# Batch 0's q of a linear-attention and expert-branch kernel: one load for each pair of heads in 1024-byte pieces, turned by products on column halves, and new durations in the planner

## The chip, the cores and the metric

The kernel runs on one core of a Trainium2 chip. The metric is the device time in microseconds (us) of one execution; times given for a kernel are the median of several executions. Engines are named as in the profile: PE is TensorE's matmul side, PEld its weight loads, DVE is VectorE, ACT is ScalarE, POOL is GpSimd, and SP is SyncE, which issues most of the DMAs.

## What is computed

```python
# q, k, v: (8 batches, 8 heads, 576 rows, 64)
kv  = np.einsum('bhsd,bhse->bhde', k, v)
out = np.einsum('bhsd,bhde->bhse', q, kv)
rms = np.sqrt(np.mean(out * out, axis=-1, keepdims=True) + 1e-06)
out = out / rms * g_norm
x = out.transpose(0, 2, 1, 3).reshape(4608, 512)
p = domain_probs / (domain_probs.sum(-1, keepdims=True) + 1e-09)   # (4608, 4)
y = sum over e of p[:, e:e+1] * (np.maximum(x @ w1[e], 0) @ w2[e])  # w1: 512x1024, w2: 1024x512
```

All of it is in float32. Attention without a softmax comes first: for each head a 64x64 product of keys and values, then the queries times it, then a normalisation over the 64 columns. Four expert branches follow, each an up product, a ReLU and a down product, mixed by the normalised domain probabilities.

## The kernel before

**The work.** The 4608 rows are cut into nine chunks of 512: the first 512 rows of each of the eight batches, and one chunk of the eight remainders of 64 rows. A stage s is one branch e on one chunk c. A stage has an up part and a down part; nearly all of them are done with a scheme of seven products of half-size blocks, nested twice, so that VectorE, ScalarE and GpSimd form many sums and differences (`combine`, L360). Stage 0 alone has a plain up part (`up_plain`, products at L999), for which only x of batch 0 and w1 of branch 0 are needed. The attention of batch 0 runs before stage 0, that of batch c+1 beside stage c.

**The attention of one batch** works on four pairs of heads. `load_pair` (from L611) loads q, k and v of a pair. For q it issues one DMA for each of the two heads: partition p gets rows 4p to 4p+3, and the two heads lie side by side inside each row block, so a row's 64 numbers, 256 bytes, are one piece. k and v are one DMA each for both heads, with 1536-byte pieces on 96 partitions. `turn` (L651) makes four 128x128 transposes on TensorE, which gives q turned with head 0 on partitions 0 to 63 and head 1 on 64 to 127; ScalarE copies that out of PSUM (L656). `key_values` (L665) makes the 64x64 products for both heads, each head in its own half of the columns; ScalarE copies them (L678). `attend` (L691) multiplies, `scaled` normalises (ScalarE squares at L564, VectorE sums at L571, GpSimd takes the power at L578 and L582, VectorE multiplies at L591), and `turn_x` (L709, copied at L717) turns the result into the layout of the products. Batch 0 has its pairs one by one, the others in two groups of two pairs. The 64 remainder rows of a batch follow the same way (L735 to L779).

**The order** is made by a planner, `Plan.layout`, before the kernel is built. Each operation has a key, which says when it is wanted, and a cost for each engine that can do it, in us. `layout` walks a clock and gives each free engine an operation. TensorE and SyncE take the first in the order of keys that can start, within a reach (0.7 of a key for TensorE); the others take the one that is due first. An operation on another engine can start 0.3 after what it needs has ended. A load ends when a modelled bus has moved it: the bus begins at 3.0 us and moves 215 KB per us, 0.5 us later the data count as landed, and at most eight loads are under way. Tiles and PSUM banks are taken from pools ("ab" and "db" have two banks each) and given back when their last reader has ended. When TensorE finds nothing to start and the first key still open on it is below 0.0, the planner adds a filler, `idle` (two transposes of the identity, L1353), with a cost of 0.23, from 1.6 us on. The order that comes out is fixed: on the chip each engine runs its list in order and waits only for semaphores. So the planner's numbers decide the order and the number of fillers, and not how long anything takes.

**The loads of branch 0's w1** are four DMAs of 512 KB (`weights_1`, from L431) in 2048-byte pieces. SyncE issues them after batch 0's q, k and v and before batch 1's.

Of the kernel before, what the change touches and what calls it, by code (L numbers as in the profile page):

```python
# [34 lines left out]
class Plan:  # L35
# [13 lines left out]

    SPARE = {"big": 6, "small": 3}  # L50
    STEP, LATE = 44.0, 20.0

    def __init__(self):
        self.ops = []
# [26 lines left out]
    def layout(self, slots, later, idle, idle_banks, idle_until):  # L81
# [20 lines left out]
                cross = self.SAME if op.cost.keys() == d.cost.keys() else self.CROSS  # L102
                d.due = min(d.due, op.due - cross - min(d.cost.values()))
        busy = {e: 0.0 for e in todo}
        bus, port = 3.0, 0.0
        lanes = [0.0] * self.LANES
        t = 0.0
        wake = [0.0, 1.6]
# [24 lines left out]
        while left:  # L133
            moved = False
            while todo["PE"] and todo["PE"][0].start is not None:
                todo["PE"].pop(0)
            front = todo["PE"][0].key if todo["PE"] else 1e9
            for eng in todo:
                if busy[eng] > t:
                    continue  # L140
                pending = todo[eng]
                while pending and pending[0].start is not None:
                    pending.pop(0)
                if not pending:
                    continue
                reach = pending[0].key + self.REACH[eng]
                best = None
                for op in pending:
                    if op.key > reach:
                        break  # L150
                    if op.start is not None:
                        continue
                    if best is not None and op.due >= best.due:
                        continue
                    when = ready(op, eng)
                    if when is None:
                        continue
                    if when > t:
                        heapq.heappush(wake, when)
                        continue  # L160
                    best = op
                    if eng in ("PE", "SP"):
                        break
                if best is not None:
                    op = best
                    op.start, op.eng = t, eng
                    if eng == "SP":
                        busy[eng] = t + op.cost[eng]
                        bus = max(bus, t + 1.5) + op.kb / 215.0
                        op.end = bus + 0.5  # L170
                        lanes = lanes[1:] + [op.end]
                    else:
                        op.end = busy[eng] = t + op.cost[eng]
                        if op.kb:
                            op.end += 9.0 if op.kb == 512 else 5.5
                    if op.port:
                        port = op.end
                        heapq.heappush(wake, port)
                    for b in op.outs:
                        if b.kind is not None and b.slot is None:  # L180
                            free[b.kind].sort()
                            b.slot = free[b.kind].pop(0)[1]
                            b.ap = slots[b.kind][b.slot]
                    for b in op.bufs:
                        b.left -= 1
                        if b.left == 0 and b.kind is not None:
                            end = max(o.end for o in [op] + b.readers + b.writers) + self.CROSS
                            free[b.kind].append((end, b.slot))
                            live[b.kind] -= 1
                            ended[b.kind] = max(end, ended.get(b.kind, 0.0))  # L190
                            for rule in [r for r in later if not any(live.get(k) for k in r[0])]:
                                later.remove(rule)
                                end = max(ended[k] for k in rule[0])
                                for ap in rule[2]:
                                    free.setdefault(rule[1], []).append((end, len(slots[rule[1]])))
                                    slots[rule[1]].append(ap)
                                heapq.heappush(wake, end)
                    heapq.heappush(wake, busy[eng])
                    heapq.heappush(wake, op.end + self.SAME)
                    heapq.heappush(wake, op.end + self.CROSS)  # L200
                    order.append(op)
                    left -= 1
                    moved = True
                if eng == "PE" and busy[eng] <= t and 1.6 <= t and front < idle_until:
                    kind, spare = next((
                        (k, f) for k in idle_banks for f in free[k] if f[0] <= t
                    ), (None, None))
                    if spare is not None:
                        op = Op(front, {"PE": 0.23}, None, (), (), 0, False)
                        op.start, op.eng, op.end = t, eng, t + 0.23  # L210
                        op.fn = lambda eng, bank=slots[kind][spare[1]]: idle(bank)
                        busy[eng] = op.end
                        free[kind].remove(spare)
                        free[kind].append((op.end, spare[1]))
                        heapq.heappush(wake, op.end)
                        order.append(op)
# [14 lines left out]
def kernel(  # L231
# [41 lines left out]
    NT = 512  # L273
# [157 lines left out]
    def weights_1(e, key, step, need):  # L431
# [4 lines left out]
        for i, (n, dh, uh) in enumerate(((1, 0, 0), (2, 1, 0), (21, 0, 1), (4, 1, 1))):  # L436
            corner[n] = Buf(None, f"w1c_{e}_{n}")
            w1corner[e][uh, dh] = f[n], corner[n]
            load(
                key + i * step, f[n],  # L440
                lambda n=n: f[n].ap[:].rearrange("p (k u) -> p k u", k=2),
                w1_src(e, dh, uh), 512, also=[corner[n]],
            )

        def form(k_, o, a, b, op):
# [155 lines left out]
    def attention(b, key, span, rem):  # L601
# [9 lines left out]
        def load_pair(hp):  # L611
            hs = slice(2 * hp, 2 * hp + 2)
            n = f"{b}_{hp}"
            kind = "kv" if b or hp < 2 else "big"
            kt, vt, qt = Buf(kind, f"k{n}"), Buf(kind, f"v{n}"), Buf("small", f"q{n}")
            want = at(hp) - 0.25 if b else key - 1 + 0.1 * hp
            for r in range(2):
                load(
                    want, qt,
                    lambda qt=qt, r=r: qt.ap[:].rearrange(  # L620
                        "p (r h d) -> p r h d", h=2, d=D)[:, :, r, :],
                    q[b, 2 * hp + r, 0:NT, :].rearrange("(p r) d -> p r d", r=NR), 128,
                )
            for t, src in ((kt, k), (vt, v)):
                load(
                    want, t,
                    lambda t=t: t.ap[0:KP, 0:2 * KR * D].rearrange("p (h x) -> p h x", h=2),
                    src[b, hs].rearrange("h (p j) d -> p h (j d)", j=KR), 288,
                )
            return kt, vt, qt  # L630

# [4 lines left out]
        for g, pairs in enumerate(groups):  # L636
# [4 lines left out]
            for o, hp in enumerate(pairs):  # L641
                kvs[hp] = kv, o
                kt, vt, qt = load_pair(hp)
                held.append((kt, vt))
                bank = Buf("ab", f"qT{b}_{hp}")
                qT = qTs[hp] = Buf("small", f"qT{b}_{hp}")

                def turn(eng, bank=bank, qt=qt):
                    for r in range(NR):
                        rs = slice(r * P, (r + 1) * P)  # L650
                        nc.tensor.transpose(bank.ap[:, rs], qt.ap[:, rs], ident[:])  # L651

                plan.add(at(hp), pe(4, P, 1), turn, reads=[qt], writes=[bank])
                plan.add(
                    at(hp), act(NT),
                    lambda eng, bank=bank, qT=qT: nc.scalar.activation(  # L656
                        out=qT.ap[:], in_=bank.ap[:], func=ACT.Copy),
                    reads=[bank], writes=[qT],
                )
# [744 lines left out]
```

## Time and profile before

| What | Value |
|---|---|
| median of 8 runs | 1723.11 us (1722.65 to 1723.87) |
| the profiled execution | 1722.65 us |
| its span | 1720.9 us |
| busy: PE, DVE, ACT, POOL | 1711.4, 1234.4, 973.5, 676.9 us |
| q loads of batch 0: two DMAs for each pair, 128 KB each | issued at 0.73, 3.29, 6.92 and 10.53 us |
| DMA rate, 2.2 to 4.5 us and 10 to 12 us | 137 and 232 GB/s |
| fillers (L1353), 0 to 30 us | 114 transposes, 57 fillers |
| four transposes of a pair's q (L651), on the chain of waits | 0.44 us |
| 24 products of keys and values of one pair (L665), on the chain of waits | 0.85 us |

The span is the profiled part of the execution; 1.75 us of the execution's time lie around it. Times of instructions are counted from the span's start. TensorE is pipelined: an instruction's own duration is longer than its distance from the next one, and on the chain of waits each group is shown with the time that it adds. A row such as "L651 PE MATMUL ab<-ident,small" names the line, the engine, the operation, the tile written and the tiles read; in brackets stands how long the engine was idle before, and what ended that.

### The profile page before, as it was taken

What the parts mean: (1) busy time and instruction counts of PE and PEld (TensorE: products, weight loads), DVE (VectorE), ACT (ScalarE), POOL (GpSimd) and SP (SyncE); (2) the same over time, 40 slices, a digit from 0 to 9 for tenths busy, and PEclk for the clock granted to TensorE, in tenths of its full rate; (3) what the DMA queues carried; (4) which work ended last, traced back from release to release, by engine and by line L of the source; (5) the groups of instructions that cost most, each with busy time, mean ns of one, the idle gap of its engine ahead of it and who ended that gap; (6) DMA issues with size and microseconds to landing.
All of it is one profiled execution on the core that took longest, in us unless ns stands there. A gap on an engine that the chain in (4) does not pass through costs nothing.

```text
span 1720.9 us, 39248 instructions
## 1 busy us (share of the span) xinstructions
PE 1711.4 (99%) x15586; PEld 1653.0 (96%) x15586; DVE 1234.4 (72%) x2034; ACT 973.5 (57%) x2378; POOL 676.9 (39%) x613
## 2 busy tenths in 40 slices
PE   9999999999999999999999999999999999999998
PEld 7699999999999999999999999999999999999998
DVE  4755655565777777777778787877788787777774
ACT  3454544454455665665666566566666666656562
POOL 2421322133335443433355544433355554433331
PEclk9999999999999999999999999999999999999999
DMA  9756444633455344444468444444478444444442
GB/s 237 224 160 194 151 118 138 194 130 117 166 146 149 106 111 105 110 112 110 127 173 191 111 111 111 111 111 111 103 183 203 115 111 111 111 111 111 102 109 49
DMA packets 156567, 230.42 MB, mean 134 GB/s; under 512 B 49888, under 2 KB 97248, under 8 KB 156384
## 3 DMA queue, kind: packets, MB, share of 16 engines
q1 hardware_dynamic: 133312, 191.21, 36.0%
q0 software_dynamic: 23072, 36.71, 14.3%
q8 instruction: 122, 2.00, 0.5%
q14 instruction: 61, 0.50, 0.1%
HBM read 154.74 MB, written 73.14 MB: 132 GB/s over the span
## 4 chain that ended last, share of the span: by engine, by line
PE 99%; POOL 1%; DVE 0%; ACT 0%; issue 0%; POOLq 0%
PE u L912 45%; PE db L1201 21%; PE ab L1201 13%; PE db L1126 12%; PE u L999 2%; PE ab L665 1%; PE ab L1353 1%; PE ab L651 1%; PE ab L709 1%; PE ab L691 1%; PE u L1126 1%; PE ab L1126 0%; POOL rt L582 0%; PE db L691 0%; PE ab L753 0%; PE ab L735 0%
## 5 line engine op out<-in xcount | busy, mean ns | idle before, releaser
L360 DVE TENSOR_TENSOR big<-big,big 128x1024 f32<-128x1024 f32 (+1 forms) x446 | 439.4, 999 | 30.6 <-ACT big L895 19.4
L912 PE MATMUL u<-xf,big 128*128 128x128 f32 x3104 | 452.4, 275 | 0.0
L912 PEld LDWEIGHTS u<-xf,big 128*128 128x128 f32 x3104 | 399.8, 192 | 1.4
L912 PE MATMUL u<-xf,w1y 128*128 128x128 f32 x2652 | 390.9, 275 | 0.0
L939 DVE TENSOR_TENSOR big<-u,snap 128x256 f32<-128x256 f32 x442 | 186.2, 421 | 232.1 <-PE u L912 162.4
L912 PEld LDWEIGHTS u<-xf,w1y 128*128 128x128 f32 x2652 | 343.2, 192 | 1.6
L931 ACT ACTIVATE snap<-u 128x256 f32<-128x256 f32 x490 | 187.8, 383 | 207.1 <-PE u L912 174.9
L931 ACT ACTIVATE big<-u 128x256 f32<-128x256 f32 x442 | 169.1, 383 | 120.0 <-PE u L912 93.3
L360 POOL TENSOR_TENSOR big<-big,big 128x256 f32<-128x256 f32 (+1 forms) x137 | 180.4, 1321 | 126.6 <-DVE big L360 61.4
L1126 PE MATMUL db<-big,big 128*128 128x256 f32 x904 | 213.8, 379 | 2.1 <-DVE big L591 2.1
L1126 PEld LDWEIGHTS db<-big,big 128*128 128x128 f32 x904 | 163.3, 190 | 19.9 <-DVE big L591 2.3
L1201 PE MATMUL db<-big,big 128*128 128x128 f32 x1204 | 166.8, 275 | 0.0
L1201 PEld LDWEIGHTS db<-big,big 128*128 128x128 f32 x1204 | 150.4, 192 | 0.1
L1229 ACT ACTIVATE snap<-db 128x256 f32<-128x256 f32 x216 | 76.8, 356 | 106.7 <-PE db L1201 103.8
L895 ACT ACTIVATE big<-big 128x1024 f32<-128x1024 f32 x128 | 134.6, 1051 | 4.0 <-DVE big L360 3.3
L1096 POOL DMA_DIRECT2D out_dram<-big x98 | 89.7, 1042 | 56.4 <-ACT big L1073 38.0
L360 POOL TENSOR_TENSOR big<-big 128x512 f32<-128x512 f32 (+1 forms) x56 | 67.7, 1209 | 108.8 <-DVE big L360 58.5
L1201 PE MATMUL ab<-kv,big 128*128 128x128 f32 x764 | 110.1, 275 | 0.0
L931 ACT ACTIVATE u<-u 128x256 f32<-128x256 f32 x245 | 90.8, 371 | 32.4 <-PE u L912 12.4
L1201 PE MATMUL db<-kv,big 128*128 128x128 f32 x752 | 109.1, 275 | 0.0
L1267 POOL TENSOR_TENSOR big<-big 128x512 f32<-128x512 f32 x25 | 31.7, 1268 | 177.6 <-DVE big L360 144.4
L578 POOL TENSOR_SCALAR ss<-ss 128x16 f32<-128x16 f32 (+2 forms) x26 | 6.4, 245 | 240.6 <-DVE ss L571 240.4
(218 smaller groups left out, 2923.8 us busy)
## 6 DMA issues: line engine op xcount, KB each, us to landing
xf<-x SPq DMA_DIRECT2D x108, 512.0 KB, 3.7
out_dram<-big POOLq DMA_DIRECT2D x82, 256.0 KB, 5.6
xf<-x_h SPq DMA_DIRECT2D x81, 256.0 KB, 3.2
xf<-x SPq DMA_DIRECT2D x81, 256.0 KB, 3.5
x<-xf SPq DMA_DIRECT2D x36, 512.0 KB, 6.3
big<-in_moe_w_dram SPq DMA_DIRECT2D x29, 512.0 KB, 6.0
small<-in_q_dram SPq DMA_DIRECT2D x72, 128.0 KB, 5.0
kv<-in_k_dram SPq DMA_DIRECT2D x30, 288.0 KB, 5.0
```

What stands on the lines that cost most here:

```text
L360: lambda eng: adder(eng).tensor_tensor(out=out_(), in0=a(), in1=b(), op=op),
L651: nc.tensor.transpose(bank.ap[:, rs], qt.ap[:, rs], ident[:])
L895: lambda eng: nc.scalar.activation(out=b.ap[:], in_=b.ap[:], func=ACT.Relu),
L912: nc.tensor.matmul(ps.ap[:, u * P:(u + 1) * P], lhsT=w1f[e][m][mm][1]()[:, u * P:(u + 1) * P], rhs=views[m][mm][1](), start=(mm in (1, 5) ...
L931: lambda eng: nc.scalar.activation(out=where(), in_=ps.ap[:, 0:HN], func=ACT.Copy),
L939: lambda eng: nc.vector.tensor_tensor(out=block(whole, a, t), in0=src.ap[:, 0:HN], in1=add_.ap[:], op=ALU.add),
L999: nc.tensor.matmul(bank.ap[:], lhsT=two(w.ap[:])[:, kt, ut * P:(ut + 1) * P], rhs=two(xh[dh].ap[:])[:, kt, :], start=(dh == kt == 0), stop ...
L1096: nc.gpsimd.dma_start(out=dst, in_=cell(i)[parts, :], accum_op=ALU.add)
L1126: nc.tensor.matmul(ps.ap[:, 0:HN], lhsT=four(h[m])[:, kt // 2, t, kt % 2, :], rhs=w2f[e][m].ap[:, kt * HN:(kt + 1) * HN], start=(m in (1, ...
L1201: nc.tensor.matmul(ps.ap[:, o * P:(o + 1) * P], lhsT=b.ap[:, col:col + P], rhs=w2q[e][m][mm][1]()[:, kt, :], start=(mm in (1, 5) and o == ...
L1229: lambda eng: nc.scalar.activation(out=where(), in_=group_of(ps.ap), func=ACT.Copy),
L1267: lambda eng: adder(eng).tensor_tensor(out=whole(to), in0=whole(a), in1=whole(b), op=ALU.add),
```

## The change

For batch 0 the two q loads of a pair become one. Partition p still gets rows 4p to 4p+3, but the heads now lie one behind the other: four rows of one head, 1024 bytes, are one piece. With that layout a row block's 128 columns of both heads are no longer side by side, so the four transposes become eight products with the identity, one for each row block and head. Each takes 64 columns as weights and writes its own half of the bank's partitions. Batches 1 to 7 keep their loads and transposes.

In the planner six numbers change. A filler costs 0.43 before 6.8 us (`SLOW`) and 0.23 after it. The bus begins at 3.8. The size that a load counts with on the bus is set to 172 for a pair's q of batch 0 (before: twice 128), to 241 for its k and v (before: 288), and to 312 for each of branch 0's four w1 blocks (before: 512). The cost of `turn` in the plan stays at `pe(4, P, 1)`.

```diff
+    SLOW = 6.8
...
-        bus, port = 3.0, 0.0
+        bus, port = 3.8, 0.0
...
-                        op = Op(front, {"PE": 0.23}, None, (), (), 0, False)
-                        op.start, op.eng, op.end = t, eng, t + 0.23
+                        took = 0.43 if t < self.SLOW else 0.23
+                        op = Op(front, {"PE": took}, None, (), (), 0, False)
+                        op.start, op.eng, op.end = t, eng, t + took
...
-                w1_src(e, dh, uh), 512, also=[corner[n]],
+                w1_src(e, dh, uh), 512 if e else 312, also=[corner[n]],
...
-            for r in range(2):
+            if b == 0:
                 load(
-                    want, qt,
-                    lambda qt=qt, r=r: qt.ap[:].rearrange(
-                        "p (r h d) -> p r h d", h=2, d=D)[:, :, r, :],
-                    q[b, 2 * hp + r, 0:NT, :].rearrange("(p r) d -> p r d", r=NR), 128,
-                )
+                    want, qt, lambda qt=qt: qt.ap[:].rearrange("p (h x) -> p h x", h=2),
+                    q[b, hs, 0:NT, :].rearrange("h (p r) d -> p h (r d)", r=NR), 172,
+                )
+            else:
...
-                    src[b, hs].rearrange("h (p j) d -> p h (j d)", j=KR), 288,
+                    src[b, hs].rearrange("h (p j) d -> p h (j d)", j=KR), 288 if b else 241,
...
-                        nc.tensor.transpose(bank.ap[:, rs], qt.ap[:, rs], ident[:])
+                        if b:
+                            nc.tensor.transpose(bank.ap[:, rs], qt.ap[:, rs], ident[:])
+                            continue
+                        for o in range(2):
+                            at = (o * NR + r) * D
+                            nc.tensor.matmul(
+                                bank.ap[o * D:(o + 1) * D, rs], lhsT=qt.ap[:, at:at + D],
+                                rhs=ident[:],
+                            )
```

More of the change, by code (lines that the diff above doesn't have):

```diff
@@ L616, in load_pair @@
             want = at(hp) - 0.25 if b else key - 1 + 0.1 * hp
-            for r in range(2):
+            if b == 0:
                 load(
-                    want, qt,
-                    lambda qt=qt, r=r: qt.ap[:].rearrange(
-                        "p (r h d) -> p r h d", h=2, d=D)[:, :, r, :],
-                    q[b, 2 * hp + r, 0:NT, :].rearrange("(p r) d -> p r d", r=NR), 128,
-                )
+                    want, qt, lambda qt=qt: qt.ap[:].rearrange("p (h x) -> p h x", h=2),
+                    q[b, hs, 0:NT, :].rearrange("h (p r) d -> p h (r d)", r=NR), 172,
+                )
+            else:
+                for r in range(2):
+                    load(
+                        want, qt,
+                        lambda qt=qt, r=r: qt.ap[:].rearrange(
+                            "p (r h d) -> p r h d", h=2, d=D)[:, :, r, :],
+                        q[b, 2 * hp + r, 0:NT, :].rearrange("(p r) d -> p r d", r=NR), 128,
+                    )
             for t, src in ((kt, k), (vt, v)):
```

## The prediction

> **What bounds the kernel now.** I read the page first, then busy time by stretch, the chain of waits over the first 80 us, and the SyncE issues with their landings.
>
> ```profile
> span 1720.9 us, 39248 instructions
> PE 1711.4 (99%) x15586; PEld 1653.0 (96%) x15586; DVE 1234.4 (72%) x2034; ACT 973.5 (57%) x2378; POOL 676.9 (39%) x613
> PE 99%; POOL 1%; DVE 0%; ACT 0%; issue 0%; POOLq 0%
> ```
>
> TensorE is the bound and idle for only 1720.9 − 1711.4 = 9.5 us. By stretch (stretch, length, busy time of PE, PEld, DVE, ACT and POOL with counts, clock, DMA share, GB/s):
>
> ```profile
> 58.00:66.00 8.00, 8.00 (x139) 5.12 (x140) 5.68 (x15) 3.51 (x8) 0.87 (x2) 1.00 0.75 179
> 66.00:75.00 9.00, 5.82 (x48) 4.92 (x44) 6.74 (x11) 2.99 (x9) 8.42 (x6) 1.00 0.84 266
> 75.00:90.00 15.00, 14.61 (x192) 12.98 (x191) 9.40 (x27) 7.70 (x18) 3.04 (x5) 1.00 0.63 202
> 90.00:120.00 30.00, 30.00 (x303) 27.99 (x303) 14.64 (x23) 15.10 (x35) 5.14 (x3) 1.00 0.61 185
> ```
>
> The idle time is 1.35 us at the start, 3.18 at 66 to 75, 0.39 at 75 to 90, and most of the rest in the tail. So an early gain survives if it shortens TensorE's queue or fills that hole; after 90 us there is nothing to wait for. The chain of waits at the opening (start, us, what):
>
> ```profile
> 1.35 6.13 PE ab L1353 x30
> 7.48 0.44 PE ab L651 x4
> 7.92 2.18 PE ab L1353 x20
> 10.10 0.85 PE ab L665 x24
> 10.95 0.37 PE ab L1353 x2
> 11.32 0.44 PE ab L651 x4
> ...
> 28.50 1.75 PE ab L1353 x16
> 30.25 0.44 PE ab L709 x4
> 30.68 3.44 PE u L999 x8
> ```
>
> L1353 is idle(), pure filler, yet it is on the chain: the data are already there. The first v is issued at 2.80 and takes 5.2 to land, so 8.0; TensorE uses it at 10.1. TensorE runs its fixed queue late, because a first-stage filler (two transposes) takes 0.41 us and the planner booked 0.23. The hole, and two stages before it:
>
> ```profile
> 27.20 1.67 SPq L366 DMA_DIRECT2D kv<-in_v_dram  x1
> 41.47 1.62 PE L665 MATMUL ab<-kv,kv 96*64 96x64 f32 x48
> 58.33 1.62 PE L665 MATMUL ab<-kv,kv 96*64 96x64 f32 x48
> 66.24 2.35 POOL L360 TENSOR_TENSOR big<-big,big 128x1024 f32<-128x1024 f32 x1 [0.70 <-ACT big L1013]
> 69.03 3.76 POOL L582 TENSOR_TENSOR rt<-ss,mhalf 128x16 f32<-128x16 f32 x1
> 73.56 1.99 PE L1126 MATMUL db<-big,big 128*128 128x256 f32 x8 [2.09 <-DVE big L591]
> ```
>
> The hole is batch 1's second attention group: its key-value product runs at 58.33, its power step ends at 72.8, and L1126 waits for its banks. The v at 27.20 takes 7.4 us to land (34.6), yet its product runs at 41.47; the last v of the second group, issued at 44.76, lands 4.7 later (49.5), its product at 58.33. Both products were ordered 7 to 9 us behind their data.
>
> **Part 1: which fillers the new constants leave.** The planner fixes order and counts, so I walk its rules by hand and take no time from it. Old constants: the bus starts at 3.0, first q ready at 3.0 + 256/215 + 0.5 + 0.3 = 4.99, TensorE free from 1.6, hence 15 fillers of 0.23. Going on so, with the two "ab" banks held until copied, gives 15, 10, 1, 1, 6, 1, 1, 6, 2, 3, 2, 1, 8 up to the last turned x: the trace's L1353 groups, x30, x20, x2, x2, x12 and so on. New constants: bus from 3.8, q 172/215 = 0.80, k and v 1.12 each; fillers 0.43 until 6.8. The pairs' q become ready at 5.40, 8.44, 11.49, 14.53 and their v at 7.64, 10.68, 13.73, 16.77. That gives 9 fillers, turn 0, 5, key-value 0, turn 1, 2, attend 0, 3, key-value 1, turn 2, 2, attend 1, 2, key-value 2, turn 3, 2, turned x 0, attend 2, key-value 3, 10, turned x 1, attend 3, 3, up, turned x 2, up, 5, turned x 3: 43 fillers for 57.
>
> **Part 2: the price of a turn.** Four transposes (0.44) become eight products, 16 instructions, since a full product of 128 columns is two (L912 x4 takes 0.45 for two products). No row has 128 rows by 64 columns with 128 moving. Upper bound: nothing overlaps, 16 × 0.111 = 1.78. Lower: the nearest row, L665, has 24 instructions of 64 moving columns on alternate halves in 0.85, 0.071 a pair; a pair can't be under the 0.111 of one 128-column instruction, so 8 × 0.111 = 0.89. I take 0.89: same halves, same alternation. The Trainium skill, "TensorE: Matmul & The Clock Gate", Terms, speaks against the change: transpose mode is 4× faster for FP32, so without it the turn would cost 1.76. The rows make one transpose half a product, not a quarter; by the rule the sum below would be some 3.5 us worse. A group leaving 64-column halves also costs 0.15 more (0.37 at 10.95 against 0.22 for two fillers after a turn); each turn now adds that.
>
> **Part 3: the new queue in traced durations.** The first-stage transposes take 421 ns, two in flight, 0.21 apart, until about 6.5, then 273 ns and 0.109 apart. Of the 30, the twelve dropped are six of each: 6 × 0.21 + 6 × 0.109 = 1.93, so turn 0 starts at 7.48 − 1.93 = 5.55. It runs slow for 1.0 us (4.7 of 8 pairs) and ends at 6.92. Ten fillers 1.24, key-value 0.85: 9.01 (before: 10.95). Turn 0.89, four 0.59, attend 0.62: 11.11 (12.60). Six 0.80, key-value: 12.76 (14.91). Turn, four, attend, four, key-value: 16.30 (18.87). Turn, four, turned x 0.44, attend 0.63, key-value: 19.70 (22.61). Twenty 2.33, turned x, attend, six: the first up at 23.90 (24.62). Up 1.72, turned x, up, ten 1.09, turned x: 29.31, against 30.68. **Gain 1.37 us.** Most of the 2.9 at 22.61 goes back into the 20 fillers that stand for batch 0's normalisation (attend to scaled x: 4.2 us for each pair in the trace, which here is always done before its turned x).
>
> How the slow stage ends, the trace shows once (421 to 273 ns at 6.5, 5.2 us after TensorE began, the clock column at 1.00). The same page of the Trainium skill (Part 1, What's actually happening) gives about 3.4 us from a free-running window, varying by run. By that the queue would be up to 0.8 us shorter. I keep 6.5: the eight runs, each with its own warm-up, lie within 1.22 us.
>
> **Part 4: the loads.** Four q DMAs fewer save four SyncE issues of about 0.6. Bytes: q-heavy stretches run at 193 GB/s (26 to 28, 894 of 993 packets under 512 B), q with k and v at 230, the 2 KB pieces of w1 at 390. So 256 KB takes 0.7 to 1.4 us; 1024-byte pieces lie nearest k's 1536, so 1.14, 0.2 saved for each pair. The start, at 137 GB/s from 2.2 to 4.5 with q alone in flight, should run at 230: 0.9 more. I cost it at nothing: landings hide behind the queue (v0 8.0 against 8.16, sooner with the gain). The cover is thinnest at key-value 3: its v lands at 20.2 in this trace and is now wanted at 18.85. The 0.8 + 0.9 earlier makes 18.5; without it TensorE waits 1.35. The new costs for w1, k and v move no byte.
>
> **Part 5: the hole.** The planner's bus ends w1 at 28.0 with the old costs, at 3.8 + 2616/215 + 4 × 312/215 = 21.8 with the new: 6.2 us earlier, and every later load in the plan with it. Up to batch 1's last v another 5832 KB follow, 27.1 us: 28.0 + 27.1 + 0.8 = 55.9, run at 58.4. Now 49.7; TensorE lags its plan by 1.8 (29.31 against 27.49), so it runs near 51.5, after the 49.5 at which the data land even now. The first group moves from 41.5 to about 33.5, for data that land at 34.6 now and at least 1 us sooner then. With key-value at 51.5 the step that ends at 73.56 (15.2 later) ends at 66.7; TensorE comes to L1126 at about 70. So of the idle 3.18 + 0.39 = 3.57 the waits on L591 (2.09) and before the turned x (0.39) go, and some 0.2 of the rest; the first up's waits for ScalarE copies stay. **Gain 2.7**, bounds 0 and 3.57. What is late next: nothing that TensorE waits for before the tail.
>
> **Sum.** 1722.65 (span 1720.9 plus 1.75 around it) − 1.37 − 2.7 = 1718.6. The median lies 0.46 above the profiled execution, so 1719.0.
>
> **Rivals.** Hole stays: SyncE or slots hold batch 1 back, and only Part 3 counts: 1723.11 − 1.37 = 1721.7. For it: k and v of the second group need the first group's four slots (SyncE sits until 42.43). Against: the first product moves too. Halves don't overlap: three turns 0.89 dearer, turn 0 0.88, 3.55 in all: 1722.6. Against: L665. Batch 1's data are late (slower): TensorE, in order, waits at L665 of batch 1. At the slowest rows, 230, 248 and 178 GB/s for the pairs' 3.4 MB, w1's 2.1 and batch 1's first 2.0, from 2.8 on and with 1.6 from byte to landing as at v0, the first group lands at 2.8 + 14.8 + 8.5 + 11.0 + 1.6 = 38.7, 5.2 after it is wanted, and the second, 3.9 MB at 178 against the 220 booked, 4.1 later: 1719.0 + 9.3 = 1728.3. It loses more than the gain once the first group lands after 37.6. Against: both products have 7 to 9 us in hand. That the smaller q pieces do nothing in themselves changes no time here; the constants do the work.
>
> **How the numbers follow.** Forecast 0.66 (1717.2 to 1720.3), hole stays 0.17, no overlap 0.09, late data 0.08. About 0.2% is what a measurement of this kernel can tell from no change: 1719.66 to 1726.56. Of the forecast 0.54 lies below, and 0.01 of the second case: faster 0.55, same 0.37, slower 0.08. The range: below, the whole 3.57 (0.87 more) and the runs' spread of 1.22, so 1716.9; above, the second and third case, so 1723.0.
>
> **What would show it.** L1353 groups of 18, 10, 4, 6, 4, 4, 4, 20, 6, 10; L651 of 16 in 0.9 us; first up near 24; L665 of batch 1 near 34 and 52; 66 to 75 without the L591 wait. It is wrong if L651 takes 1.8 us, if L665 waits for a DMA, or if a new wait of several us stands between 30 and 90.

## The result and the profile after

| | Before | After |
|---|---|---|
| median, executions | 1723.45 us, 32 | 1718.26 us, 12 |
| lowest and highest | 1722.65, 1725.03 | 1717.01, 1719.82 |
| the profiled execution | 1722.65 us | 1718.86 us |
| its span | 1720.9 us | 1717.1 us |

The ratio of the times is 0.9971, with a 95% interval of 0.9964 to 0.9979: the kernel is faster by 0.3%, some 5 us. The page of the profile after:

```profile
span 1717.1 us, 39296 instructions
PE 1709.6 (100%) x15606; PEld 1651.3 (96%) x15606; DVE 1230.8 (72%) x2023; ACT 973.6 (57%) x2378; POOL 691.2 (40%) x624
PE 97%; POOL 1%; DMA 1%; DVE 0%; SPq 0%; issue 0%; ACT 0%; POOLq 0%
```

TensorE has 20 instructions more: four turns with 16 in place of 4 add 48, and 28 filler transposes are gone. It is busy 1.8 us less, and idle for 7.5 us in place of 9.5. Busy time by stretch (stretch, length, then busy time of PE, PEld, DVE, ACT and POOL with counts, clock, DMA share, GB/s), for the stretches shown of before:

```profile
58.00:66.00 8.00, 8.00 (x27) 3.85 (x28) 6.43 (x16) 3.07 (x7) 7.31 (x6) 1.00 0.95 280
66.00:75.00 9.00, 7.53 (x93) 6.83 (x92) 6.98 (x14) 4.75 (x12) 3.90 (x3) 1.00 0.49 175
75.00:90.00 15.00, 15.00 (x167) 14.24 (x168) 8.98 (x25) 8.82 (x21) 8.09 (x8) 1.00 0.94 305
90.00:120.00 30.00, 30.00 (x302) 27.29 (x301) 16.38 (x26) 12.29 (x29) 8.32 (x6) 1.00 0.43 129
```

At 66 to 75 TensorE works for 7.53 of 9 us, before for 5.82, and at 75 to 90 it no longer waits at all. The chain of waits at the opening, in the execution after (start, us, what):

```profile
2.22 6.75 DMA small<-in_q_dram
...
8.99 8.12 DMA small<-in_q_dram
...
17.15 1.09 PE ab L664 x16
...
20.74 2.33 PE ab L1369 x20
...
24.94 1.72 PE u L1015 x4
...
28.82 1.09 PE ab L1369 x10
29.91 0.44 PE ab L725 x4
```

Before, this chain ran through TensorE's own fillers from 1.35 us on. Now it follows two q loads up to 17.11: the shorter queue has caught up with its data. (L664 is the new product of the turn, L1369 the filler, L725 the turned x, L1015 the plain up product, L681 the products of keys and values, L1142 the down product, L593 the last step of `scaled`.) The hole, in the timeline of the same execution:

```profile
35.17 1.62 PE L681 MATMUL ab<-kv,kv 96*64 96x64 f32 x48
52.65 1.62 PE L681 MATMUL ab<-kv,kv 96*64 96x64 f32 x48
65.07 2.92 POOL L584 TENSOR_TENSOR rt<-ss,mhalf 128x16 f32<-128x16 f32 x1
68.76 1.99 PE L1142 MATMUL db<-big,big 128*128 128x256 f32 x8 [1.47 <-DVE big L593]
```

Batch 1's products of keys and values run 6.3 and 5.7 us earlier than before; the power step of its second group ends at 67.99, where it ended at 72.8, and L1142 still waits, for 1.47 in place of 2.09 us.

**Where the 3.8 us between the two profiled executions come from.** The end of the same instruction in both traces, side by side, shows it. The last turned x of batch 0 ends at 30.34 in place of 30.68: 0.34 won in the opening. From 113 us on the distance is a constant 3.56, up to 1688 us; so 3.22 were won between. The last 0.25 come in the tail.

The hole has to be counted by what the groups add to the chain, not by idle time. The timeline of before has these two beside the down product at 73.56:

```profile
70.76 0.71 PE L912 MATMUL u<-big,w1y 128*128 128x128 f32 x4
76.77 0.66 PE L709 MATMUL ab<-ident,big 128*128 128x128 f32 x4 [0.39 <-ACT big L717]
```

Its chain of waits has the same work where nothing holds it up:

```profile
77.43 1.73 PE db L1126 x8
89.20 2.68 PE u L912 x24
```

The 28 instructions of L912 from 66.4 to 71.47 added 5.12 us; at 2.68 for 24 they need 3.13. The eight of L1126 behind them added 4.09 for 1.73, and a turned x 1.05 for 0.44. Together that is 4.95 us lost, while TensorE was idle for 3.57 only: an instruction's own duration is longer than what it adds, and so covers a part of a wait. After, the same account gives 3.47 − 1.73 = 1.74. The difference is the 3.2.

### The profile page after: what moved, and what is told of

Same layout as the page of the kernel before. It is cut to its first block, busy times and chain, and to the rows that moved or that the text cites. A ratio compares the mean times of both kernels' runs of the same rounds, so it can differ in the third digit from the quotient of the medians.

```text
span 1717.1 us, 39296 instructions
## 1 busy us (share of the span) xinstructions
PE 1709.6 (100%) x15606; PEld 1651.3 (96%) x15606; DVE 1230.8 (72%) x2023; ACT 973.6 (57%) x2378; POOL 691.2 (40%) x624
## 4 chain that ended last, share of the span: by engine, by line
PE 97%; POOL 1%; DMA 1%; DVE 0%; SPq 0%; issue 0%; ACT 0%; POOLq 0%
PE u L928 45%; PE db L1217 21%; PE ab L1217 13%; PE db L1142 12%; PE ab L681 1%; DMA small<-in_q_dram 1%; PE u L1015 1%; PE ab L725 1%; PE ab L707 1%; PE ab L660 1%; PE u L1142 1%; POOL rt L584 0%; PE ab L1142 0%; POOL big L362 0%; POOL ss L580 0%; PE ab L1369 0%
## 5 line engine op out<-in xcount | busy, mean ns | idle before, releaser
L362 POOL TENSOR_TENSOR big<-big,big 128x256 f32<-128x256 f32 (+1 forms) x139 | 185.1, 1337 | 122.8 <-DVE big L362 55.5
L1142 PE MATMUL db<-big,big 128*128 128x256 f32 x904 | 213.9, 379 | 1.5 <-DVE big L593 1.5
L1142 PEld LDWEIGHTS db<-big,big 128*128 128x128 f32 x904 | 163.2, 190 | 19.2 <-DVE big L593 1.7
```

Of the source, the lines that this page charges most:

```text
L362: lambda eng: adder(eng).tensor_tensor(out=out_(), in0=a(), in1=b(), op=op),
L1142: nc.tensor.matmul(ps.ap[:, 0:HN], lhsT=four(h[m])[:, kt // 2, t, kt % 2, :], rhs=w2f[e][m].ap[:, kt * HN:(kt + 1) * HN], start=(m in (1, ...
```

## The experiments

The table sets all kernels side by side. "Slow until" is the start of the last instruction of the opening that took over 350 ns, in the profiled execution. "Last x" is the end of batch 0's last turned x. "Attend" is the distance from there to the attention products of batch 1's second group. "Hole" is the time lost between last x and the first deep down product, counted as above (4.95 in the profile of before; in the others, by how much longer or shorter that stretch is). So the span is that of before plus the differences of "last x" and "hole", but for some 0.3 us.

| Kernel | Median us (executions) | Ratio, 95% interval | Filler transposes | Slow until | Last x | Attend | Hole |
|---|---|---|---|---|---|---|---|
| before | 1723.45 (32) | 1 | 114 | 6.52 | 30.68 | 32.06 | 4.95 |
| before_again | 1723.33 (1) | | 114 | 4.39 | 29.66 | 32.06 | 6.64 |
| e2_layout | 1725.44 (11) | 1.0013, 1.0004 to 1.0021 | 114 | 5.46 | 32.98 | 32.06 | 4.97 |
| e4_fillers | 1721.77 (11) | 0.9990, 0.9981 to 0.9999 | 100 | 5.46 | 29.01 | 32.06 | 4.95 |
| e8_kv_w1_old | 1722.37 (11) | 0.9995, 0.9986 to 1.0003 | 88 | 6.30 | 29.88 | 31.85 | 7.11 |
| e9_turn_cost | 1718.03 (6) | 0.9968, 0.9956 to 0.9979 | 74 | 4.61 | 29.18 | 30.10 | 1.80 |
| e10_fillers_w1 | 1717.67 (5) | 0.9966, 0.9953 to 0.9978 | 100 | 5.89 | 28.89 | 29.14 | 1.77 |
| e5_w1_only | 1718.25 (6) | 0.9971, 0.9959 to 0.9982 | 114 | 3.96 | 29.45 | 28.82 | 1.44 |
| e3_w1_512 | 1717.42 (5) | 0.9966, 0.9952 to 0.9979 | 86 | 4.60 | 29.47 | 28.37 | 0.99 |
| e1_constants | 1719.27 (11) | 0.9979, 0.9970 to 0.9987 | 86 | 5.70 | 32.24 | 26.45 | 3.36 |
| e1_again | 1718.95 (1) | | 86 | 4.18 | 30.23 | 26.45 | 1.69 |
| e6_halves_in_turn | 1719.61 (11) | 0.9978, 0.9969 to 0.9987 | 86 | 5.03 | 31.28 | 26.44 | 3.42 |
| after | 1718.26 (12) | 0.9971, 0.9964 to 0.9979 | 86 | 6.51 | 30.34 | 26.45 | 1.73 |
| after_again | 1718.05 (6) | 0.9968, 0.9956 to 0.9980 | 86 | 4.39 | 29.43 | 26.45 | 1.74 |

### The new numbers alone, on the old loads and turns (e1_constants)

```diff
+    SLOW = 6.8
-        bus, port = 3.0, 0.0
+        bus, port = 3.8, 0.0
...
+                        took = 0.43 if t < self.SLOW else 0.23
...
-                w1_src(e, dh, uh), 512, also=[corner[n]],
+                w1_src(e, dh, uh), 512 if e else 312, also=[corner[n]],
...
-                    q[b, 2 * hp + r, 0:NT, :].rearrange("(p r) d -> p r d", r=NR), 128,
+                    q[b, 2 * hp + r, 0:NT, :].rearrange("(p r) d -> p r d", r=NR), 128 if b else 86,
...
-                    src[b, hs].rearrange("h (p j) d -> p h (j d)", j=KR), 288,
+                    src[b, hs].rearrange("h (p j) d -> p h (j d)", j=KR), 288 if b else 241,
```

> All the new planner numbers on the kernel before; q of batch 0 keeps its two loads of 256-byte pieces for each pair (86 on the bus each, 172 together) and its four transposes. Theory A (the numbers do the work, the new q layout costs): the hole at 66 to 75 us closes as in the changed kernel, and the turns cost less: the trace of the changed kernel spends 5.07 us in batch 0's turns, four of the old ones 0.44 to 0.59 each, so 2.9 less; about 1715.5 us, 1714.5 to 1717.5, and below the changed kernel. Theory B (the larger pieces and the single load do the work): 1721 to 1724 us, and the 66 to 75 hole of 3.2 us is still there.

The median is 1719.27, 4.25 us below before (1723.52 in 27 executions beside it) and not below after. The profiled execution, the slowest of the eleven (1722.65), shows two losses. The waits of its TensorE over the first 30 us (what waited, for what, us in total, times, longest):

```profile
PE ab L653 <- DMA small<-in_q_dram: 2.8, 3, 2.0
...
PE ab L667 <- DMA kv<-in_v_dram: 0.2, 1, 0.2
```

The turn (L653 here) waits 2.8 us for q in 256-byte pieces. The second loss is the hole: 3.36 us, although the order there is that of after. Behind the longest wait for q, and again behind the wait at the hole, the granted clock stood at 0.5 for 3.41 us; the last part comes back to that. So the four turns of 0.44, which should have saved 4 × 0.44 against after, don't reach the end: the old loads are too late for this queue. My expectation that the numbers alone would do better than the whole change fell.

### The new load and turn alone, with the old numbers (e2_layout)

```diff
-            for r in range(2):
+            if b == 0:
                 load(
-                    want, qt,
-                    lambda qt=qt, r=r: qt.ap[:].rearrange(
-                        "p (r h d) -> p r h d", h=2, d=D)[:, :, r, :],
-                    q[b, 2 * hp + r, 0:NT, :].rearrange("(p r) d -> p r d", r=NR), 128,
+                    want, qt, lambda qt=qt: qt.ap[:].rearrange("p (h x) -> p h x", h=2),
+                    q[b, hs, 0:NT, :].rearrange("h (p r) d -> p h (r d)", r=NR), 256,
...
+                        for o in range(2):
+                            at = (o * NR + r) * D
+                            nc.tensor.matmul(
...
```

> The new q load and the new turn on the old planner numbers (q counted with its true 256 KB). Theory A: slower than the kernel before by the dearer turns, four times about 0.5 to 0.8 us, with 57 or so fillers as before: 1725.5 us, 1724 to 1727, hole still there. Theory B: 1718 to 1720.5 us.

The median is 1725.44, 1.9 us above before. The order on TensorE is that of before, with all 114 filler transposes. The four turns add 4.10 us in place of 1.91, and the hole is as it was (by stretch, same columns as above):

```profile
66.00:75.00 9.00, 6.69 (x59) 4.65 (x48) 7.10 (x10) 4.29 (x11) 6.75 (x4) 1.00 1.04 322
75.00:90.00 15.00, 13.75 (x182) 12.15 (x183) 9.68 (x28) 7.14 (x17) 3.75 (x6) 1.00 0.51 158
```

The last v of batch 0 landed at 14.72 in place of 20.27. In a queue that is fixed, data that land earlier move nothing, and a dearer turn shows in full. By itself the part that gives the change its name costs time.

### After, with the old size for w1 (e3_w1_512)

```diff
-                w1_src(e, dh, uh), 512 if e else 312, also=[corner[n]],
+                w1_src(e, dh, uh), 512, also=[corner[n]],
```

> The changed kernel with w1 of branch 0 at 512 on the planner's bus, as before, everything else new. Theory A (w1's number alone brings batch 1's attention forward and so closes the hole): the first key-value product of batch 1 goes back from 35 to about 39 us or later, the hole at 66 to 75 comes back, 2 to 3 us: 1721 us, 1720 to 1722. Rival (the hole is closed by the earlier opening, or by the k, v and q numbers): 1718 to 1719 us.

I had put the whole gain of the hole down to this number. That fell: 1717.42, as fast as after, and the hole is smaller than in any other kernel:

```profile
66.00:75.00 9.00, 8.88 (x66) 8.02 (x68) 7.82 (x14) 5.26 (x13) 4.36 (x4) 1.00 0.79 280
75.00:90.00 15.00, 15.00 (x200) 13.96 (x197) 10.46 (x25) 6.68 (x16) 4.67 (x6) 1.00 0.98 330
```

Batch 1's products of keys and values stand at 36.62 and 53.48 here. The smaller sizes for q, k and v, even with the later bus start, already end w1 on the planner's bus at 25.5, which is 2.5 us earlier than before, and that is enough.

### The filler cost and the bus start alone, on before (e4_fillers)

```diff
+    SLOW = 6.8
-        bus, port = 3.0, 0.0
+        bus, port = 3.8, 0.0
...
+                        took = 0.43 if t < self.SLOW else 0.23
```

> The kernel before with only the filler's 0.43 before 6.8 us and the bus from 3.8. Theory A: only the opening gains: the first fillers fall from 15 to 10 (2 us on TensorE), the plan runs 0.8 later, so about 1.5 us gained by the first up, the hole stays at 3 us: 1722 us, 1721 to 1723. Rival (an earlier opening by itself pulls all that follows with it and closes the hole too): 1718 to 1720 us.

1721.77, 1.75 us below before, with the hole untouched at 4.95: the gain is that of the opening, with 14 filler transposes less and the old turns. Six of the eleven executions had a mean granted clock of 1.000, with a median of 1721.03; the other five, at 0.997 to 0.999, have one of 1722.74. That is taken up with the last experiment.

### The size of w1 alone, on before (e5_w1_only)

```diff
-                w1_src(e, dh, uh), 512, also=[corner[n]],
+                w1_src(e, dh, uh), 512 if e else 312, also=[corner[n]],
```

> The kernel before with one number changed: branch 0's w1 at 312 on the planner's bus. Its TensorE order is that of the kernel before up to the last turned x, 57 fillers; after that it leaves three of the plain up products behind the attend of batch 1's second group, where the kernel before leaves one and the changed kernel four. Theory A (the hole closes because the order leaves work to cover the normalisation of that group; nothing else is needed): the 3.57 us idle at 66 to 90 us fall below 1 and the time by about 3: 1720.5 us, 1719.5 to 1721.5. Rival (the hole closes only together with the earlier opening): 1723 to 1724 us.

1718.25: this one number gives as much as the whole change, and the time lies below the 1719.5 to 1721.5 expected. The hole fell by 3.51, where about 3 had been expected. The opening is 1.23 shorter in the profile, although its order is the same: the slow start ended at 3.96 and not at 6.52. TensorE's first 30 us are those of before, fillers, turns and all. At the place of the hole its timeline shows the down product (L1126) without a wait in brackets:

```profile
68.44 1.89 PE L1126 MATMUL db<-big,big 128*128 128x256 f32 x8
72.52 1.89 PE L1126 MATMUL db<-big,big 128*128 128x256 f32 x8
```

So w1's number is enough, and by e3_w1_512 it isn't needed: what has to happen is that the planner thinks that its bus is free for batch 1 earlier, whichever load it believes smaller.

### The products of the turn sorted by head (e6_halves_in_turn)

```diff
-                        for o in range(2):
...
+                    for o in range(2):
+                        for r in range(NR):
```

> The changed kernel with the eight products of a turn sorted by head: four on the lower columns, then four on the upper ones. Same plan, same order of everything else. Theory A (products on alternate halves overlap in pairs, and only neighbours do): a warm turn goes from 0.88 to about 1.7 us, batch 0's turns together about 3 us longer, and since the fillers are fixed the kernel too: 1721 us, 1720 to 1722. Rival (the overlap doesn't hang on the alternation, the queue or the weight load sets the pace): 0.9 us a turn still, 1717.5 to 1719 us.

The eight products of one head's half, then those of the other. The chain of waits of this kernel:

```profile
13.80 1.36 PE ab L666 x16
...
17.81 1.36 PE ab L666 x16
```

A turn takes 1.36 where heads that alternate take 0.88 (turn 1 of after); all three stand directly behind products of keys and values, and none waits. That lies between the two values expected: sorted halves overlap in part. The median, 1719.61, is 1.35 above after and a little under the 1720 to 1722 expected.

### After, with the old sizes for w1 and for batch 0's k and v (e8_kv_w1_old)

```diff
-                w1_src(e, dh, uh), 512 if e else 312, also=[corner[n]],
+                w1_src(e, dh, uh), 512, also=[corner[n]],
...
-                    src[b, hs].rearrange("h (p j) d -> p h (j d)", j=KR), 288 if b else 241,
+                    src[b, hs].rearrange("h (p j) d -> p h (j d)", j=KR), 288,
```

> The changed kernel with k and v of batch 0 at 288 and w1 at 512 on the planner's bus again; the new q load, the turn, q at 172, the bus from 3.8 and the fillers stay. Its order leaves one plain up product behind the attend of batch 1's second group, as in the kernel before. Theory A (that cover decides): 2 to 3.5 us idle at 66 to 90 us again, 1721.5 us, 1720 to 1723. Rival (any of the new numbers closes it): 1717 to 1719 us.

The hole is back and so is the time: 1722.37. On the planner's bus w1 ends at 27.25 here (28.0 before, 28.8 in e4_fillers, 25.5 in e3_w1_512, 24.3 in e5_w1_only, 21.8 after). Between 25.5 and 27.25 the order changes. The column "attend" shows it on the chip: where the second attention of batch 1 stands 31.85 or 32.06 us behind the last turned x, one plain up product is left behind it, and the hole is 5 to 7 us; at 30.1 there are two left, at 28.4 to 29.1 three, at 26.4 four, and the hole is 1 to 1.8 us, or 3.4 in two executions. Each plain product is 1.9 us of work for TensorE while VectorE and GpSimd normalise.

### A turn planned at the price of eight products, w1 at its old size (e9_turn_cost)

```diff
-                w1_src(e, dh, uh), 512 if e else 312, also=[corner[n]],
+                w1_src(e, dh, uh), 512, also=[corner[n]],
...
-                plan.add(at(hp), pe(4, P, 1), turn, reads=[qt], writes=[bank])
+                plan.add(at(hp), pe(4 if b else 8, P, 1), turn, reads=[qt], writes=[bank])
```

> The changed kernel with w1 back at 512 on the planner's bus, the better of the runs so far at 1717.4, and the turn of batch 0 planned at its true 0.90 in place of 0.45. The plan then drops 12 of the 86 fillers' transposes, 1.3 us, and leaves one plain product behind the attend of batch 1's second group plus one more behind the remainder. Theory A (the opening is now set by the landing of q and v at turns 2 and 3, so fewer fillers buy little, and the smaller cover costs 1 to 2): 1718 us, 1717 to 1719.5. Rival (the opening is still set by TensorE's own list): 1716 us.

The planner drops 12 filler transposes more (74), and the time stays where it was, 1718.03 beside 1717.42 of e3_w1_512 with overlapping intervals. TensorE now waits 0.7 us for v at the first products of keys and values and 0.6 for q at the turns, and the last turned x ends at 29.18 (29.47), with a slow start that ended at the same 4.6. So 12 transposes, 1.3 us in the plan, buy 0.29: the data bind now. The hole takes that back, 1.80 for 0.99; the order leaves two plain products behind the attention in place of three.

### The filler cost, the bus start and w1's size, on before (e10_fillers_w1)

```diff
+    SLOW = 6.8
-        bus, port = 3.0, 0.0
+        bus, port = 3.8, 0.0
...
-                w1_src(e, dh, uh), 512, also=[corner[n]],
+                w1_src(e, dh, uh), 312 if e == 0 else 512, also=[corner[n]],
```

> The kernel before with three planner numbers changed and nothing of the loads or turns: the filler at 0.43 before 6.8 us, the bus from 3.8, branch 0's w1 at 312. Its order leaves three plain up products behind the attend of batch 1's second group, as with w1 alone (1718.25 us), and has 100 fillers' transposes for 114. Theory A (two separate gains, the filler's 1.7 us measured with it alone and w1's 5.2): 1716.5 us, 1715.5 to 1717.5, below the changed kernel. Rival (in the opening the loads of 256-byte pieces bind as soon as fillers go): 1718 to 1719 us.

1717.67, with none of the new load or turn. Its last turned x ends at 28.89, although the slow stage lasted until 5.89; after_again has 29.43 with one that ended at 4.39. The gains of e4_fillers (1.75) and e5_w1_only (5.2) add to 5.7 and not to 6.9, and the kernel can't be told from after: their intervals overlap. So the new load and turn aren't needed for the time that after reaches.

### After, the numbers and before, each once more (after_again, e1_again, before_again)

> The changed kernel once more, beside the last candidate and for a second trace. Theory A: the order and the waits are the same, and what differs from the first trace is when the slow first stage of TensorE ends (6.5 us there, 3.7 to 6.5 in the other runs) and whether the clock falls in the 1.5 us wait before L1142; 1718.3 us, 1717.5 to 1719. Rival: the opening's gain of 0.3 us in the first trace is what the change gives there, whatever the clock: the last turned x of batch 0 again at 29.9.

> The new planner numbers on the old loads and turns once more, one look: its first profile fell on its slowest run (1722.65, median 1719.3). Theory A (the 256-byte pieces land too late for the shorter queue): TensorE waits for q of pair 2 or 3 before turns at 12 to 19 us, 1 to 2.5 us in all, where the changed kernel waits 0.8; time 1718 to 1720. Rival (the first profile's waits were that run's alone): under 0.8 us of waits.

> The kernel before once more, one look, for a second trace. The medians differ by 5.2 us, the first two traces by 3.8. Theory A (before's profile was its fastest run: in its usual one the clock falls to half in or after the 2.1 us wait at 71 to 74 us, as it does after the waits of e6_halves_in_turn and e8_kv_w1_old): a granted clock under 1.00 between 70 and 78 us where the time is 1723.4 or more, 1 to 2 us more added there; the last turned x of batch 0 near 29 where the slow first stage of TensorE ends near 4 us, as with w1 alone. Rival (the difference lies in the steady part or around the span): the clock 1.00 all through and the same 4.95 us lost at 66 to 77 us.

**after_again**: 1718.05, span 1716.2. The slow stage ended at 4.39 in place of 6.51, and the first up came at 24.03 in place of 24.94. The wait for L593 is 1.47 again.

**e1_again**: 1718.95. The waits of its first 30 us, in the same view as above:

```profile
PE ab L653 <- DMA small<-in_q_dram: 0.9, 3, 0.4
PE ab L667 <- DMA big<-in_v_dram: 0.7, 2, 0.5
PE ab L667 <- DMA kv<-in_v_dram: 0.6, 1, 0.6
```

Less than in the first profile, and spread over q and v. So the numbers alone leave a queue that hangs on the old loads by an amount that differs between executions: the eleven of e1_constants reach from 1718.22 to 1722.65, those of after from 1717.01 to 1719.82 and of after_again from 1717.11 to 1718.65. By the medians the old loads cost some 1 us against after, with intervals that overlap.

**before_again**: 1723.33, span 1721.6. Its slow stage ended 2.1 us sooner than in the first profile of before and its last turned x 1.02 sooner, yet its span is 0.7 longer. By stretch, and the down product in its timeline:

```profile
70.00:72.00 2.00, 0.45 (x4) 0.26 (x3) 1.01 (x2) 0.22 (x1) 1.92 (x2) 1.00 0.95 283
72.00:74.00 2.00, 1.46 (x4) 1.19 (x5) 1.63 (x4) 0.00 (x0) 1.92 (x3) 0.74 0.08 17
74.00:76.00 2.00, 2.00 (x7) 1.49 (x6) 1.01 (x3) 0.02 (x1) 1.59 (x3) 0.50 0.08 31
76.00:78.00 2.00, 1.61 (x13) 1.28 (x12) 0.00 (x0) 1.65 (x4) 0.00 (x0) 0.90 1.01 296
```

```profile
72.55 3.40 PE L1126 MATMUL db<-big,big 128*128 128x256 f32 x8 [2.10 <-DVE big L591]
```

The wait is the same as in the first profile, 2.10 us against 2.09, but behind it the granted clock (the column after POOL's) falls to 0.74 and 0.50, and the eight products take 3.40 in place of 1.99. The hole costs 6.64 us, 1.69 more than in the first profile. Against after_again the accounts are then: opening 0.23, hole 4.90, tail 0.25, together 5.4; the spans differ by 1721.6 − 1716.2 = 5.4 and the medians by 5.2.

The same 1.7 us stands elsewhere: e1_constants less e1_again 3.36 − 1.69, e6_halves_in_turn less after 3.42 − 1.73, both with a drop of the clock in the first of the two; and in e4_fillers 1722.74 − 1721.03 between executions with and without it. Of 60 executions of before that ran beside the experiments, 51 had a mean granted clock below 1.000; of 19 of after and after_again, 3. So in this pair of traces the change gains by the hole twice: the wait is shorter, and the clock holds.

How much of the 5.2 between the medians is the clock's isn't shown. Within one kernel the executions with and without a drop can lie closer than 1.7: in before the 51 have a median of 1723.49, the nine others 1722.75, and in e6_halves_in_turn five below 1.000 have 1719.57, six others 1719.65. In the two traces of before, the drop comes with the slow start that ended sooner, 1.69 − 1.02 = 0.67 together, which fits the 0.74; whether the other executions pair the two so, no run shows. The nine of before without a drop still lie 4.7 above after_again.

## The prediction, step by step

**Part 1, the fillers: right.** The groups of L1369 in the trace are 18, 10, 4, 6, 4, 4, 4, 20, 6, 10, as forecast. Fillers add 12.84 us in place of 16.06.

**Part 2, the turn: right, but for where it stands.** A turn with its data there and at full speed, turn 1, takes 0.88; forecast 0.89. By an estimate from the rule of the Trainium skill, "TensorE: Matmul & The Clock Gate", Terms, on transposes in FP32 it would have been 1.76; the rows, which make a transpose half a product, decided rightly. Directly behind fillers a turn takes 1.02 (all four in e2_layout, turn 0 in after_again); the forecast charged 0.15 for leaving the column halves and nothing for entering them. e6_halves_in_turn shows that the alternation mattered too: the price holds only while the halves alternate.

**Part 3, the opening: the term of 1.37 us measured 0.34.** The end of the slow stage was taken right for this execution (6.51), and that was luck: in after_again it came at 4.39, and the fourteen profiles reach from 3.96 to 6.52. (6 × 0.21 + 6 × 0.109 is 1.91 and not 1.93, which changes nothing here.) What is missing stands group by group: turn 0 took 1.68 for 1.38, the ten fillers behind it 1.36 for 1.24, turn 2 took 1.19 and turn 3 took 1.33, for 0.89 each; turn 0 started 0.1 earlier than forecast. Together 0.30 + 0.12 + 0.30 + 0.44 − 0.1 = 1.06, for the 1.03 missing. Some half of turn 0's excess is the price of standing behind fillers. Four turns came to 5.07 us where 1.91 stood: 3.16 more, against the 3.22 that the fillers give. Two turned x that add 0.44 in place of 0.59 are what is left of the gain. With the slow stage ending early in both, after_again against before_again, it is 0.23.

**Part 4, the loads cost nothing: wrong at two places, and not at the one named.** The cover was said to be thinnest at key-value 3, whose v landed at 19.41; it ran at 19.89 and didn't wait. The turns of pairs 2 and 3 did: the queue came to them at 13.08 and 16.92, and their q landed at 13.13 and 17.11. A wait of 0.10 and one of 0.23 cost 0.30 and 0.44, some 0.2 more than the idle time each. My sum had the start at 230 GB/s and the rest at 230 too. The start ran at 283, but from 7 to 16 us the bus moved 218, where it moved 235 before, while the queue came to these turns 2.2 and 3.6 us sooner (15.28 and 20.51 before). That rate isn't the load's own: in e2_layout the same loads moved 302 GB/s from 7 to 16 us, and this q had landed at 9.70 and 12.63. Why the rate differs stays open. e2_layout and e1_constants part the two: without the shorter queue the new load gives nothing back for its dearer turns; with it the old one costs 2.2 to 3.0 us of waits.

**Part 5, the hole: the cause as put, the sizes off.** The products of keys and values of batch 1 came at 35.17 and 52.65 (forecast 33.5 and 51.5), the normalisation ended at 68.72 (66.7), and TensorE came to L1142 at 67.29 (70). So the wait for L593 didn't go, it shrank to 1.47; and yet the gain was 3.2 for 2.7. The step that failed is the bound: "of the idle 3.57" took the busy share for the loss, and the loss was 4.95. The reason given, w1's end on the planner's bus 6.2 us earlier, is what happens, but far more than needed: 2.5 us do it (e3_w1_512).

**Rivals.** The hole stays: it didn't, after; in e8_kv_w1_old and e4_fillers it did. The halves don't overlap: 0.88 says no. Batch 1's data late: L681 ran 0.90 and 1.98 us behind the landings of the last v of its two groups (34.27 and 50.67), where it had 7 to 9 us before. It didn't wait, but most of the cover is used.

**The sum.** 1718.6 was worked out for the profiled execution and 1718.86 measured: opening 1.03 too much, hole 0.5 and tail 0.25 too little. That the sum comes so close is luck, since these errors cancel. The median was 0.7 below the 1719.0 for two reasons. The 0.46 by which the first profile of before lay under its median doesn't carry over: its profiled execution was one in which the clock held behind the hole, as in nine of 60. And the profile of after lies 0.60 above its own median, with a slow start that ended late.

## What to carry to other kernels

In a kernel whose order is fixed ahead, look for a planner's number that places work 7 to 9 us behind its data: correcting one load's size was worth as much here as a new load, a new turn and six numbers together (e5_w1_only). Count a hole by the time that instructions add to the chain, not by idle time, and ask whether the clock holds behind it. A faster load can pay only when the queue has become short enough to wait for it (here some 1 us, not clear of the noise), and what it costs in instructions is paid at once.

## What the hardware showed

**The slow start ends where it likes.** The first transposes take 421 ns and then 273, with the clock column at 1.00 all along. The change came 3.96 to 6.52 us after the span's start in fourteen profiled executions, and the same kernel has both: before 6.52 and 4.39, after 6.51 and 4.39. It moves the last turned x by about 1 us. The Trainium skill, "TensorE: Matmul & The Clock Gate", What's actually happening, ascribes this to a window of about 3.4 us that runs freely and so varies by run; the spread, 2.6 us, agrees with that in kind, while the page speaks of ±0.5 us.

**A short wait can cost the clock.** One wait of 2.10 us, with two of 0.52 and 0.57 in the 6 us ahead of it, was followed by a granted clock of 0.5 in one profile of before and not in the other; in e6_halves_in_turn a wait of 1.47 us was:

```profile
70.00:72.00 2.00, 2.00 (x6) 1.60 (x5) 2.00 (x3) 0.00 (x0) 0.83 (x1) 0.51 0.02 8
72.00:74.00 2.00, 2.00 (x11) 1.61 (x11) 1.99 (x5) 0.62 (x2) 0.00 (x0) 0.64 0.34 131
```

```profile
69.70 3.48 PE L1144 MATMUL db<-big,big 128*128 128x256 f32 x8 [1.47 <-DVE big L593]
```

TensorE has no idle time in these 4 us and still takes 3.48 for what takes 1.99 in after, behind the same wait. The same section of that page asks for at least one idle window, some 3.4 us, before the clock falls; these waits are shorter, and the measurement decides. In the clock records the drop in e6_halves_in_turn, and each of the two in e1_constants, lasts 3.41 us, as does that in before_again (by stretch, same columns):

```profile
72.98:76.38 3.40, 3.40 (x12) 2.64 (x10) 1.66 (x5) 0.40 (x1) 2.61 (x4) 0.50 0.17 66
```

The one in e8_kv_w1_old lasts 6.83, twice that. They begin at 72.98 in before_again, 19.59 and 70.79 in e1_constants, 70.04 in e6_halves_in_turn and 71.50 in e8_kv_w1_old. Counted from "slow until" in the same execution, these are 20, 4, 19, 19 and 19 steps of 3.41 us and 0.2 to 0.4 us more. So in these four executions the end of the slow start and the drops keep one and the same beat of 3.41 us, and where that beat lies differs between executions. That would be a part of what picks the executions in which the clock falls; the rest stays open. In after_again, too, the wait of 1.47 us (66.39 to 67.86) lay between two such points, and the clock held.

**Larger pieces had no rate of their own.** From 2.2 to 4.5 us the seven profiles with the new load ran at 274 to 305 GB/s, the seven with 256-byte pieces at 137 to 178. The pieces aren't all of that: with one DMA in place of two, k and v were issued 0.9 and 1.1 us sooner. From 7 to 16 us, beside k and v, the old loads ran at 234 to 245. The new ones ran at 302 in e2_layout, 268 in e9_turn_cost and 210 to 234 in the other five, after among them, although e2_layout and after issue the same loads at the same times, within 0.02 us, up to 5.6 us. Why the rate differs no run tells.
